# Second attention of a fused attention and two-layer-pair kernel: from one chunk at a time to sets of two or four chunks, turned by VectorE and DMAs

## The chip, the cores and the metric

The kernel runs on one core of a Trainium2 chip. The metric is the device time in microseconds (us). One launch computes everything; the host only lays the inputs out and turns the output back.

## The reference

All of it is float32, with N = 12480 tokens, C = 128 channels, 32 inducing vectors and FF = 2048. The inputs x, inducing, both matrices of the first pair and the first one of the second are drawn as below and multiplied by 8.

```python
def mab(q, kv):                       # attention without projections
    s = scale * (q @ kv.T); s = s - s.max(-1)
    a = exp(s); a /= a.sum(-1) + 1e-09
    return a @ kv
h = mab(inducing, x)                  # first attention: 32 rows over all tokens
x = mab(x, h)                         # second attention: every token over 32 rows
t = x @ w_in;  x = maximum(0.01*t, t) @ w_out            # first pair
t = x @ w_in2                                            # second pair
g = where(t >= 1, t, where(t <= -1, 0, (t + 1)**2 / 4))
y = g @ w_out2
```

## The kernel before, in words

Channels and hidden units lie on the 128 partitions, tokens along the free dimension. The first attention goes over all tokens in nine bands and ends at some 46 us with `HT`, the 32 rows, channel by row. Then the 12480 tokens are worked off in 25 chunks, ten of 504 and fifteen of 496 tokens (`WIDTHS`), and each chunk's 2048 hidden units in 16 blocks of 128 (`NJ`). A step k of the main loop is one such block, c, j = divmod(k, 16). The order of all instructions on each engine is the order in which the program is written.

In a step four stages stand beside each other, each for a block of its own:

- Stage 1 (while k < 400): one product `Gs` x `aT` for block k into a bank of `b1`. `aT` holds the second attention's weights of chunk c, 96 rows by tokens: low parts, high parts, high parts again (32 rows each). `Gs` is `HT` times the first matrix. ScalarE takes the high part (`hi`, L565), VectorE the low part (`lo`, L572); in four steps of sixteen GpSimd does the latter (L570), after a copy `r` by ScalarE.
- Stage 2, four steps behind: three products into `px` (bank 0 or 1 by the chunk's parity, `bX`). At the end of a chunk come one more product with `Qs` and the split into `x2hi` and `x2lo` (L619, L620).
- Stage 3, from k = 86 on, for block kb = k - 86: three products into one of the three banks `b3`. VectorE clamps (`cl`, L597), ScalarE squares (`sq`, L577), VectorE adds (`g`, L603), ScalarE takes the high part (L584) and GpSimd the low part (`lo`, L589).
- Stage 4, five blocks behind stage 3: three products into `py`; at a chunk's end a copy and a DMA to `out_y`.

So a step has 4 products for k < 86, 7 for k = 86 to 90, 10 up to k = 400, and 6 afterwards. All of these are issued by `mm` (L516). Before k = 86 (called the fill below) the weights of three matrices are converted as well, on VectorE, ScalarE and GpSimd (`convert`, L96 to L124).

The second attention of chunk c + 1 is made during chunk c by `attend`, one part at the end of each of some steps. Chunks 0 to 6 are scored by token: four products with the chunk's tokens as weights put 126 tokens on the partitions and 4 x 32 scores along them (L470, 4 products in 8 passes). Chunks 7 to 24 are scored by row (L448, likewise 8 passes), copied by ScalarE (L452) and turned by TensorE (L455). Then VectorE takes the maximum (L476) and the difference (L478), ScalarE the exponential (L481), VectorE sum, reciprocal and product (L485 to L488), ScalarE the high part (L492), VectorE the low part (L495), TensorE turns both in four products with an identity (L501), and ScalarE copies the turned rows out of PSUM (L506, L508). The bank is `bX[c % 2]`. `ATTEND` and `ATTEND_G` name the steps j of a chunk in which the parts stand. All DMAs go through the SP queue. At k = 86 the pools of the fill are closed and their memory is used by stages 3 and 4.

Of the kernel before, what the change touches and what calls it, by code (L numbers as in the profile page):

```python
# [31 lines left out]
SCALE = 1.0 / math.sqrt(C)  # L32
EPS = 1e-9
# [37 lines left out]
def moe_kernel(ctx: ExitStack, tc, x_d, xf_d, xl_d, xt_d, it_d, w1_d, w2_d, w3_d, w4_d, y_d):  # L71


    nc = tc.nc
# [8 lines left out]
    xp = ctx.enter_context(tc.tile_pool(name="xp", bufs=2))  # L83
    ps = ctx.enter_context(tc.tile_pool(name="ps", bufs=1, space=PSUM))
# [81 lines left out]

    xts = {}

    def load_xt(c):
        t = xp.tile([C, CW], F32, name="xt")  # L170
        nc.sync.dma_start(out=t[:, :WIDTHS[c]], in_=xt_d[:, AT[c]:AT[c + 1]])
        xts[c] = t

# [12 lines left out]
    xb, xT = {}, {}  # L186
# [24 lines left out]
    ident = const.tile([128, 128], F32, name="ident")  # L211
# [24 lines left out]
    HT = const.tile([C, 3, M], F32, name="HT")  # L236
# [85 lines left out]
    for s in range(NS_B):  # L322
# [14 lines left out]
        if s == NS_B - 3:  # L337
# [31 lines left out]
                            in1=rden[:, None, :].to_broadcast([C, 3, M]), op=ALU.mult)  # L369
# [9 lines left out]
    at = ctx.enter_context(tc.tile_pool(name="at", bufs=2))  # L379
    ap = ctx.enter_context(tc.tile_pool(name="ap", bufs=2))  # L380
# [3 lines left out]
    bX = (bank[0], bank[1])  # L384
# [3 lines left out]
    x2, h1, aT, st = {}, {}, {}, {}  # L388
# [49 lines left out]

    def scores_g(c, part):

        b = bX[c % 2]
        bt = WIDTHS[c] // CB
        if part == 0:
            t = xts.pop(c)
            if c + 1 < NCH:
                load_xt(c + 1)
            for q in range(CB):
                nc.tensor.matmul(b[q * M:(q + 1) * M, :bt], lhsT=HT[:, 0, :], rhs=t[:, q * bt:(q + 1) * bt],  # L448
                                 start=True, stop=True)
        elif part == 1:  # L450
            s = at.tile([128, BT], F32, name="sT")
            nc.scalar.activation(s[:, :bt], b[:, :bt], AF.Copy)  # L452
            st[c] = s[:, :bt]
        else:
            nc.tensor.transpose(b[:bt, 128:256], st[c], ident)  # L455

    def attend(c, part):

        b = bX[c % 2]
        bt = WIDTHS[c] // CB  # L460
        if c >= GROUPS:
            if part < 3:
                return scores_g(c, part)
            part -= 2
        if part == 0:
            t = xts.pop(c)
            if c + 1 < NCH:
                load_xt(c + 1)
            for q in range(CB):
                nc.tensor.matmul(b[:bt, q * M:(q + 1) * M], lhsT=t[:, q * bt:(q + 1) * bt], rhs=HT[:, 0, :],  # L470
                                 start=True, stop=True)
        elif part == 1:
            at0 = 128 if c >= GROUPS else 0
            sv = b[:bt, at0:at0 + CB * M].rearrange("p (b m) -> p b m", m=M)
            m = at.tile([BT, CB], F32, name="m")[:bt]
            nc.vector.tensor_reduce(out=m, in_=sv, op=ALU.max, axis=AX.X)  # L476
            e = at.tile([BT, CB, M], F32, name="ea")[:bt]
            nc.vector.tensor_tensor(out=e, in0=sv, in1=m[:, :, None].to_broadcast([bt, CB, M]), op=ALU.subtract)  # L478
            st[c] = e
        elif part == 2:  # L480
            nc.scalar.activation(st[c], st[c], AF.Exp, scale=SCALE)  # L481
        elif part == 3:
            e = st[c]
            d = at.tile([BT, CB], F32, name="d")[:bt]
            nc.vector.tensor_reduce(out=d, in_=e, op=ALU.add, axis=AX.X)  # L485
            nc.vector.tensor_scalar(out=d, in0=d, scalar1=EPS, scalar2=None, op0=ALU.add)
            nc.vector.reciprocal(out=d, in_=d)
            nc.vector.tensor_tensor(out=e, in0=e, in1=d[:, :, None].to_broadcast([bt, CB, M]), op=ALU.mult)  # L488
        elif part == 4:
            e = st[c]  # L490
            s = at.tile([BT, CB, 3, M], F32R, name="s")[:bt]
            nc.scalar.activation(s[:, :, 1, :], e, AF.Copy)  # L492
            if c == 0:
                nc.scalar.activation(s[:, :, 2, :], e, AF.Copy)
            nc.vector.tensor_tensor(out=s[:, :, 0, :], in0=e, in1=s[:, :, 1, :].bitcast(F32), op=ALU.subtract)  # L495
            st[c] = s
        elif part == 5:
            s = st.pop(c)
            r = 2 if c else 3
            for q in range(CB):  # L500
                nc.tensor.matmul(b[:r * M, q * bt:(q + 1) * bt], lhsT=s[:, q, :r].rearrange("p r m -> p (r m)"),  # L501
                                 rhs=identr[:bt, :bt], start=True, stop=True)
        elif part == 6:
            t = ap.tile([K1, CW], F32R, name="aT")[:, :CB * bt]
            r = 2 if c else 3
            nc.scalar.activation(t[:r * M], b[:r * M, :CB * bt], AF.Copy)  # L506
            if c:
                nc.scalar.activation(t[2 * M:], b[M:2 * M, :CB * bt], AF.Copy)  # L508
            aT[c] = t

    def mm(out, w, x, start, stop):

        n = x.shape[1]
        cuts = [n * i // PARTS for i in range(PARTS + 1)]
        for i, (a, b) in enumerate(zip(cuts, cuts[1:])):
            nc.tensor.matmul(out[:, a:b], lhsT=w, rhs=x[:, a:b], start=start and i == 0, stop=stop and i == PARTS - 1)  # L516

# [21 lines left out]
    work(WORK_T[3])  # L539

    NS = NCH * NJ
    for k in range(NS + LAG * NJ + OB + D2):
        c, j = divmod(k, NJ)
        kb = k - LAG * NJ - OB
        cb, jb = divmod(kb, NJ)
# [5 lines left out]
        if kb == 0:  # L551
# [4 lines left out]
            ep = ctx.enter_context(tc.tile_pool(name="ep", bufs=3))  # L556
        steps = ATTEND_G if c + 1 >= GROUPS else ATTEND
        part = steps.index(j) if j in steps and c + 1 < NCH else None
# [63 lines left out]
        if 0 <= ky < NS:  # L622
# [9 lines left out]
        if part is not None:  # L632
            attend(c + 1, part)
        if k in HIDDEN:
# [59 lines left out]
```

## Time and profile before

| | |
|---|---|
| time, median of 3 runs | 1009.83 us (1009.11 to 1010.76) |
| time of the profiled execution | 1012.33 us |
| its span, first to last instruction | 1010.5 us |
| TensorE busy, share of the span | 995.8 us, 99% |
| VectorE / ScalarE / GpSimd busy | 830.0 / 826.1 / 643.8 us |

The span is what the views of the profile show; 1.8 us of the profiled execution lie outside it. A product is shown longer than the time for which it holds TensorE, since the products overlap; the distance from the start of one to the start of the next tells what it costs.

### The profile page before, as it was taken

Reading aid. Unit: us, or ns where it says so; the run is one execution under the profiler, and the core shown is the slowest. Engines: PE = TensorE matmul, PEld = TensorE weight load, DVE = VectorE, ACT = ScalarE, POOL = GpSimd, SP = SyncE. Lnnn points to the kernel's source line nnn. Section 1 sums busy time; section 2 is a strip of 40 time slices with the busy share of each in tenths; the row PEclk is TensorE's granted clock in tenths of the full one; section 3 lists DMA queues with packets and bytes.
Section 4 is the critical chain, followed back from the end, with each engine's and each line's share of the span. In section 5 each row is a group of like instructions: output and inputs, shape, how many; then the busy total and the mean of one; then the engine's idle time right before and its main releaser. Section 6 shows DMA issues by size and latency. Waiting matters only on the chain.

```text
span 1010.5 us, 15224 instructions
## 1 busy us (share of the span) xinstructions
PE 995.8 (99%) x4858; PEld 806.2 (80%) x4858; DVE 830.0 (82%) x1442; ACT 826.1 (82%) x1556; POOL 643.8 (64%) x513
## 2 busy tenths in 40 slices
PE   8899999999999999999999999999999999999998
PEld 6567777888888888888888888888888888888886
DVE  5768998888888888888878878878878878789997
ACT  5577788888888888888888888888888888889987
POOL 0034466667667666666666666666666666678886
PEclk9999999999999999999999999999999999999999
DMA  9700000000000000000000000000000000000000
GB/s 357 311 15 11 21 12 11 12 10 21 14 8 21 18 4 21 22 1 21 21 1 22 21 1 21 20 1 21 21 1 21 12 1 11 11 11 11 11 11 21
DMA packets 11232, 29.86 MB, mean 30 GB/s; under 512 B 1376, under 2 KB 7776, under 8 KB 10384
## 3 DMA queue, kind: packets, MB, share of 16 engines
q1 hardware_dynamic: 11152, 28.89, 8.0%
q8 instruction: 38, 0.62, 0.3%
q14 instruction: 42, 0.34, 0.1%
HBM read 22.50 MB, written 6.39 MB: 29 GB/s over the span
## 4 chain that ended last, share of the span: by engine, by line
PE 93%; DVE 3%; ACT 2%; POOL 1%; issue 1%; POOLq 0%; ACTq 0%
PE bank L516 86%; PE bank L255 1%; ACT hi L565 1%; DVE lo L572 1%; PE bank L267 1%; PE bank L300 1%; PE bank L501 1%; PE bank L448 1%; PE bank L470 1%; DVE ea L488 0%; PE bank L318 0%; PE bank L225 0%; PE bank L395 0%; PE bank L289 0%; DVE cva L109 0%
## 5 line engine op out<-in xcount | busy, mean ns | idle before, releaser
L589 POOL TENSOR_TENSOR lo<-g,hi 128x496 fp32r<-128x496 f32 (+1 forms) x392 | 497.4, 1272 | 228.3 <-PE bank L516 162.1
L565 ACT ACTIVATE hi<-bank 128x496 fp32r<-128x496 f32 (+1 forms) x400 | 233.4, 590 | 122.6 <-PE bank L516 119.8
L516 PE MATMUL bank<-lo,whi 128*128 128x496 f32 (+1 forms) x800 | 310.4, 388 | 1.5 <-POOL lo L570 1.5
L516 PE MATMUL bank<-hi,whi 128*128 128x496 f32 (+1 forms) x800 | 310.7, 388 | 0.0
L516 PE MATMUL bank<-hi,wlo 128*128 128x496 f32 (+1 forms) x800 | 310.3, 388 | 0.0
L577 ACT ACTIVATE sq<-cl,half 128x496 f32<-128x496 f32 (+1 forms) x400 | 284.2, 711 | 12.3 <-DVE cl L597 5.5
L597 DVE TENSOR_SCALAR cl<-bank 128x496 f32<-128x496 f32 (+1 forms) x400 | 268.2, 670 | 27.6 <-PE bank L516 22.0
L603 DVE SCALAR_TENSOR_TENSOR g<-bank,sq 128x496 f32<-128x496 f32 (+1 forms) x400 | 267.8, 669 | 25.7 <-ACT sq L577 24.2
L572 DVE SCALAR_TENSOR_TENSOR lo<-bank,hi 128x496 fp32r<-128x496 f32 (+1 forms) x305 | 203.7, 674 | 92.8 <-ACT hi L565 92.7
L584 ACT ACTIVATE hi<-g 128x496 fp32r<-128x496 f32 (+1 forms) x400 | 245.7, 614 | 0.7 <-DVE g L603 0.5
L516 PEld LDWEIGHTS bank<-lo,whi 128*128 128x128 f32 x800 | 150.3, 188 | 34.2 <-POOL lo L570 3.2
L516 PEld LDWEIGHTS bank<-hi,wlo 128*128 128x128 f32 x800 | 150.5, 188 | 30.2
L516 PEld LDWEIGHTS bank<-hi,whi 128*128 128x128 f32 x800 | 150.5, 188 | 30.0 <-ACT y L630 0.4
L516 PE MATMUL bank<-aT,Gs 96*128 96x496 f32 (+1 forms) x400 | 164.1, 411 | 0.8 <-ACT aT L506 0.8
L570 POOL TENSOR_TENSOR lo<-r,hi 128x496 fp32r<-128x496 f32 (+1 forms) x95 | 122.9, 1294 | 64.9 <-ACT r L569 61.3
L516 PE MATMUL bank<-x2hi,whi 128*128 128x496 f32 (+1 forms) x400 | 156.1, 390 | 0.7 <-DVE g L603 0.7
L516 PE MATMUL bank<-x2hi,wlo 128*128 128x496 f32 (+1 forms) x400 | 155.4, 389 | 0.0
L516 PE MATMUL bank<-x2lo,whi 128*128 128x496 f32 (+1 forms) x400 | 155.2, 388 | 0.0
L516 PEld LDWEIGHTS bank<-aT,Gs 96*128 96x128 f32 x400 | 75.3, 188 | 21.2 <-issue 4.5
L516 PEld LDWEIGHTS bank<-x2hi,wlo 128*128 128x128 f32 x400 | 75.9, 190 | 14.9
L516 PEld LDWEIGHTS bank<-x2hi,whi 128*128 128x128 f32 x400 | 75.9, 190 | 14.4 <-DVE g L603 1.5
L516 PEld LDWEIGHTS bank<-x2lo,whi 128*128 128x128 f32 x400 | 75.2, 188 | 15.3
(120 smaller groups left out, 537.7 us busy)
## 6 DMA issues: line engine op xcount, KB each, us to landing
wraw<-in_w SPq DMA_DIRECT2D x16, 512.0 KB, 9.9
xb<-in_x SPq DMA_DIRECT2D x5, 1024.0 KB, 14.2
xt<-in_xt SPq DMA_DIRECT2D x15, 248.0 KB, 2.7
out_y<-y SPq DMA_DIRECT2D x15, 248.0 KB, 2.0
xt<-in_xt SPq DMA_DIRECT2D x10, 252.0 KB, 2.7
out_y<-y SPq DMA_DIRECT2D x10, 252.0 KB, 2.1
xl<-in_xl SPq DMA_DIRECT2D x1, 1024.0 KB, 15.2
xb<-in_x SPq DMA_DIRECT2D x2, 256.0 KB, 8.4
```

The source lines that it names most:

```text
L255: nc.tensor.transpose(ps_t[:, i * p:(i + 1) * p], xb[s][:, q, b, :], ident[:p, :p])
L267: nc.tensor.matmul(p[q * M:(q + 1) * M, :w], lhsT=iT, rhs=xT[s][:, q * w:(q + 1) * w], start=True, stop=True)
L300: nc.tensor.matmul(A[q * M:(q + 1) * M], lhsT=eTs[s][:p, b * 128 + q * M:b * 128 + (q + 1) * M], rhs=xb[s][:, q, b, :], start=(b == 0), st ...
L516: nc.tensor.matmul(out[:, a:b], lhsT=w, rhs=x[:, a:b], start=start and i == 0, stop=stop and i == PARTS - 1)
L565: nc.scalar.activation(hi, p1, AF.Relu)
L570: nc.gpsimd.tensor_tensor(out=lo, in0=r, in1=hi.bitcast(F32), op=ALU.subtract)
L572: nc.vector.scalar_tensor_tensor(out=lo, in0=p1, scalar=0.0, in1=hi.bitcast(F32), op0=ALU.max, op1=ALU.subtract)
L577: nc.scalar.activation(sq, cl, AF.Square, scale=-0.5, bias=half)
L584: nc.scalar.activation(hi, g, AF.Copy)
L589: nc.gpsimd.tensor_tensor(out=lo, in0=g, in1=hi.bitcast(F32), op=ALU.subtract)
L597: nc.vector.tensor_scalar(out=cl, in0=p3, scalar1=1.0, scalar2=-1.0, op0=ALU.min, op1=ALU.max)
L603: nc.vector.scalar_tensor_tensor(out=g, in0=b3[(kb - 1) % 3][:, :w], scalar=-1.0, in1=sq, op0=ALU.max, op1=ALU.add)
```

## The change

The first three chunks (0 to 2) are still scored by token, one at a time. The other 22 are done in seven sets: two of 2 chunks, four of 4 and one of 2. A set's part p stands at the end of step first + p, for p from 0 to 11. The scores are made by row for the whole set, four products of n x 128 columns. VectorE turns them in blocks of 32 x 32 out of PSUM, so that each partition holds tokens and 32 scores lie next to each other. Maximum, difference, sum and product are done on n x 128 elements a partition, now from SBUF, the exponential and the high part by ScalarE; high and low parts are turned back by the same kind of VectorE instruction, and twelve DMAs a set (SBUF to SBUF, 32 partitions and runs of 125 floats each) spread them into the 96 rows of `aTg`. TensorE turns nothing in a set, and ScalarE copies nothing out of PSUM.

Chunks are now 488, 496, 496 and 22 times 500 tokens. The x of a set is laid out by the host in quarters of 128 tokens (125 and the next three) and loaded in one DMA, of 1 MB for four chunks. The set of step 89 is loaded at k = 86, into memory of the fill. Chunks 1 and 2 have their high parts copied twice by ScalarE before the turn, as chunk 0 had, and so one copy out of PSUM.

```diff
-WIDTHS = (504,) * 10 + (496,) * 15
+WIDTHS = (488, 496, 496) + (500,) * 22
+TB = 128
+SINGLE = 3
+SETS = ((3, 2, 15), (5, 2, 36), (7, 4, 89), (11, 4, 150), (15, 4, 214), (19, 4, 278), (23, 2, 342))
+PARTS = 12
+FEW, MANY = 2, 4
...
+    def attend_set(i, part):
+        c, n, k = SETS[i]
+        b = bX[(k // NJ + 1) % 2]
+        w = n * TB
...
+        def spread(t, r, v):
+            v = v.rearrange("p (n t) -> p n t", t=TB)
+            for q in range(CB):
+                nc.sync.dma_start(out=t[r * M:(r + 1) * M, :n, q * bt:(q + 1) * bt].bitcast(F32),
+                                  in_=v[q * M:(q + 1) * M, :, :bt])
+        if part == 0:
+            t = xts.pop(c)
+            for q in range(CB):
+                nc.tensor.matmul(b[q * M:(q + 1) * M, :w], lhsT=HT[:, 0, :], rhs=t[:, :, q, :], start=True, stop=True)
+            if i + 1 < len(SETS) and (late_pools or SETS[i + 1][2] < kb0):
+                load_xt(*SETS[i + 1][:2])
+        elif part == 1:
+            nc.vector.transpose(out=e, in_=b[:, :w])
+        elif part == 2:
+            nc.vector.tensor_reduce(out=m, in_=blocks(st[c]), op=ALU.max, axis=AX.X)
+        elif part == 3:
+            nc.vector.tensor_tensor(out=blocks(e), in0=blocks(e), in1=wide(m), op=ALU.subtract)
+        elif part == 4:
+            nc.scalar.activation(st[c], st[c], AF.Exp, scale=SCALE)
+        elif part == 5:
+            nc.vector.tensor_reduce(out=d, in_=blocks(e), op=ALU.add, axis=AX.X)
+            nc.vector.tensor_scalar(out=d, in0=d, scalar1=EPS, scalar2=None, op0=ALU.add)
+            nc.vector.reciprocal(out=d, in_=d)
+        elif part == 6:
+            nc.vector.tensor_tensor(out=blocks(e), in0=blocks(e), in1=wide(d), op=ALU.mult)
+        elif part == 7:
+            nc.scalar.activation(hi, st[c], AF.Copy)
+        elif part == 8:
+            nc.vector.transpose(out=hT, in_=hi.bitcast(F32))
+        elif part == 9:
+            for r in (1, 2):
+                spread(t, r, hT)
+        elif part == 10:
+            nc.vector.tensor_tensor(out=lo, in0=e, in1=hi.bitcast(F32), op=ALU.subtract)
+            nc.vector.transpose(out=lT, in_=lo.bitcast(F32))
+        else:
+            spread(t, 0, lT)
...
+        for i, (_, _, first) in enumerate(SETS):
+            if 0 <= k - first < PARTS:
+                attend_set(i, k - first)
```

## Rows read from the trace of the kernel before

**Rows 1.** The page, chain that ended last, shares of the span by engine.

```profile
PE 93%; DVE 3%; ACT 2%; POOL 1%; issue 1%; POOLq 0%; ACTq 0%
```

**Rows 2.** Busy time by engine, one chunk of the fill, one later chunk.

```profile
core 0: us, PE busy (x) PEld busy (x) DVE busy (x) ACT busy (x) POOL busy (x), PEclk, DMA share, GB/s
92.76:110.51 17.75, 16.97 (x78) 13.08 (x78) 17.08 (x30) 13.86 (x29) 9.76 (x7) 1.00 0.06 16
211.26:249.00 37.74, 37.74 (x175) 30.62 (x174) 30.85 (x53) 31.58 (x60) 25.40 (x21) 1.00 0.05 15
```

**Rows 3.** TensorE in order of time, steps of ten products: start, duration, line.

```profile
500.50 0.39 PE L516 MATMUL bank<-lo,whi 128*128 128x504 f32 x1
500.97 0.40 PE L516 MATMUL bank<-x2hi,whi 128*128 128x504 f32 x1
...
505.06 0.39 PE L516 MATMUL bank<-lo,whi 128*128 128x504 f32 x1
505.82 0.40 PE L516 MATMUL bank<-x2hi,whi 128*128 128x504 f32 x1
...
563.36 0.39 PE L516 MATMUL bank<-lo,whi 128*128 128x496 f32 x1
564.36 0.39 PE L516 MATMUL bank<-x2hi,whi 128*128 128x496 f32 x1
...
568.40 0.38 PE L516 MATMUL bank<-lo,whi 128*128 128x496 f32 x1
568.96 0.39 PE L516 MATMUL bank<-x2hi,whi 128*128 128x496 f32 x1
```

**Rows 4.** TensorE in order of time, scores of the first attention.

```profile
24.77 1.04 PE L267 MATMUL bank<-xT,iT 128*32 128x512 f32 x8
25.74 0.66 PE L289 MATMUL bank<-ident,e 128*128 128x128 f32 x4
```

**Rows 5.** Groups by line and shape, VectorE: busy us, mean ns, idle before.

```profile
L495 DVE TENSOR_TENSOR s<-ea,s 124x128 fp32r<-124x128 f32 x15 | 20.8, 1387 | 0.0
...
L608 DVE TENSOR_TENSOR lo<-g,hi 128x496 fp32r<-128x496 f32 x8 | 5.3, 667 | 0.2 <-ACT hi L584 0.2
...
L488 DVE TENSOR_TENSOR ea<-ea,d 124x128 f32<-124x128 f32 x15 | 4.4, 292 | 0.5
```

**Rows 6.** All engines in order of time, end of a step of ten products.

```profile
573.24 1.26 POOL L589 TENSOR_TENSOR lo<-g,hi 128x496 fp32r<-128x496 f32 x1 [1.05 <-PE bank L516]
573.26 0.67 DVE L603 SCALAR_TENSOR_TENSOR g<-bank,sq 128x496 f32<-128x496 f32 x1
...
575.49 0.39 PE L516 MATMUL bank<-aT,Gs 96*128 96x496 f32 x1
```

**Rows 7.** All engines in order of time, steps of the fill.

```profile
98.32 0.39 PE L516 MATMUL bank<-aT,Gs 96*128 96x504 f32 x1
...
98.85 0.67 DVE L620 TENSOR_TENSOR x2lo<-bank,x2hi 128x504 fp32r<-128x504 f32 x1
...
99.58 1.07 PE L470 MATMUL bank<-HT,xt 128*126 128x32 f32 x8 [0.17 <-DVE x2lo L620]
100.48 0.48 PE L516 MATMUL bank<-aT,Gs 96*128 96x504 f32 x1
...
105.14 0.40 PE L516 MATMUL bank<-aT,Gs 96*128 96x504 f32 x1
...
106.05 0.39 PE L516 MATMUL bank<-aT,Gs 96*128 96x504 f32 x1
...
107.64 0.45 PE L516 MATMUL bank<-aT,Gs 96*128 96x504 f32 x1
...
151.49 0.39 PE L516 MATMUL bank<-lo,whi 128*128 128x504 f32 x1
...
152.51 0.47 PE L516 MATMUL bank<-aT,Gs 96*128 96x504 f32 x1
```

**Rows 8.** The page, DMA issues: count, size, median us from issue to landing.

```profile
xt<-in_xt SPq DMA_DIRECT2D x15, 248.0 KB, 2.7
```

More of the change, by code (lines that the diff above doesn't have):

```diff
@@ L167, in moe_kernel, with load_xt @@
     xts = {}
[L169 to L172, printed above, removed]
+    late_pools = {}
+    def load_xt(c, n=1):
+        if n == 1:
+            t = xp.tile([C, CB * TB], F32, name="xt", bufs=2)
+        elif n == FEW and not late_pools:
+            t = xp.tile([C, FEW * CB * TB], F32, name="xts")[:, :n * CB * TB]
+        else:
+            t = late_pools["x"].tile([C, MANY * CB * TB], F32, name="xtm")[:, :n * CB * TB]
+        nc.sync.dma_start(out=t, in_=xt_d[:, c * CB * TB:(c + n) * CB * TB])
+        xts[c] = t.rearrange("p (n q t) -> p n q t", q=CB, t=TB)
     iT = const.tile([C, M], F32, name="iT")
@@ L437, in linear, with tile_of, blocks, wide @@
             nc.vector.tensor_tensor(out=lo, in0=b[M:2 * M, :C], in1=lo.bitcast(F32), op=ALU.subtract)
-    def scores_g(c, part):
+    def attend_set(i, part):
+        c, n, k = SETS[i]
+        b = bX[(k // NJ + 1) % 2]
+        pool = late_pools["a"] if late_pools else at
+        most = MANY if late_pools else FEW
+        w = n * TB
+        bt = WIDTHS[c] // CB
+        def tile_of(name, dtype=F32):
+            return pool.tile([128, most * TB], dtype, name=name)[:, :w]
+        def blocks(t):
+            return t.rearrange("p (b m) -> p b m", m=M)
+        def wide(t):
+            return t[:, :, None].to_broadcast([128, n * CB, M])
+        def spread(t, r, v):
[10 more added lines that the diff above has]
+        elif part == 1:
+            e = tile_of("eg")
+            nc.vector.transpose(out=e, in_=b[:, :w])
+            st[c] = e
+        elif part == 2:
+            m = pool.tile([128, most * CB], F32, name="mg")[:, :n * CB]
+            nc.vector.tensor_reduce(out=m, in_=blocks(st[c]), op=ALU.max, axis=AX.X)
+            st[c] = st[c], m
+        elif part == 3:
+            e, m = st[c]
+            nc.vector.tensor_tensor(out=blocks(e), in0=blocks(e), in1=wide(m), op=ALU.subtract)
+            st[c] = e
+        elif part == 4:
+            nc.scalar.activation(st[c], st[c], AF.Exp, scale=SCALE)
+        elif part == 5:
+            e = st[c]
+            d = pool.tile([128, most * CB], F32, name="dg")[:, :n * CB]
+            nc.vector.tensor_reduce(out=d, in_=blocks(e), op=ALU.add, axis=AX.X)
+            nc.vector.tensor_scalar(out=d, in0=d, scalar1=EPS, scalar2=None, op0=ALU.add)
+            nc.vector.reciprocal(out=d, in_=d)
+            st[c] = e, d
+        elif part == 6:
+            e, d = st[c]
+            nc.vector.tensor_tensor(out=blocks(e), in0=blocks(e), in1=wide(d), op=ALU.mult)
+            st[c] = e
+        elif part == 7:
+            hi = tile_of("hg", F32R)
+            nc.scalar.activation(hi, st[c], AF.Copy)
+            st[c] = st[c], hi
+        elif part == 8:
+            e, hi = st[c]
+            hT = tile_of("hT")
+            nc.vector.transpose(out=hT, in_=hi.bitcast(F32))
+            st[c] = e, hi, hT
+        elif part == 9:
+            e, hi, hT = st[c]
+            t = (late_pools["t"] if late_pools else ap).tile([K1, most, CW], F32R, name="aTg")
+            for r in (1, 2):
+                spread(t, r, hT)
+            st[c] = e, hi, t
+        elif part == 10:
+            e, hi, t = st[c]
+            lo = tile_of("lg", F32R)
+            nc.vector.tensor_tensor(out=lo, in0=e, in1=hi.bitcast(F32), op=ALU.subtract)
+            lT = tile_of("lT")
+            nc.vector.transpose(out=lT, in_=lo.bitcast(F32))
+            st[c] = lT, t
+        else:
+            lT, t = st.pop(c)
+            spread(t, 0, lT)
+            for i in range(n):
+                aT[c + i] = t[:, i, :]
@@ L441, in scores_g, with attend @@
+    def attend(c, part):
         b = bX[c % 2]
@@ L444, in scores_g @@
             t = xts.pop(c)
-            if c + 1 < NCH:
+            if c + 1 < SINGLE:
                 load_xt(c + 1)
+            if c == 0:
+                load_xt(*SETS[0][:2])
             for q in range(CB):
-                nc.tensor.matmul(b[q * M:(q + 1) * M, :bt], lhsT=HT[:, 0, :], rhs=t[:, q * bt:(q + 1) * bt],
+                nc.tensor.matmul(b[:bt, q * M:(q + 1) * M], lhsT=t[:, 0, q, :bt], rhs=HT[:, 0, :],
                                  start=True, stop=True)
         elif part == 1:
[L451 to L474, printed above, removed]
+            sv = b[:bt, :CB * M].rearrange("p (b m) -> p b m", m=M)
             m = at.tile([BT, CB], F32, name="m")[:bt]
@@ L498, in attend @@
             s = st.pop(c)
-            r = 2 if c else 3
             for q in range(CB):
-                nc.tensor.matmul(b[:r * M, q * bt:(q + 1) * bt], lhsT=s[:, q, :r].rearrange("p r m -> p (r m)"),
+                nc.tensor.matmul(b[:K1, q * bt:(q + 1) * bt], lhsT=s[:, q].rearrange("p r m -> p (r m)"),
                                  rhs=identr[:bt, :bt], start=True, stop=True)
         elif part == 6:
[L504 to L508, printed above, removed]
+            t = ap.tile([K1, CW], F32R, name="aT0")[:, :CB * bt]
+            nc.scalar.activation(t, b[:K1, :CB * bt], AF.Copy)
             aT[c] = t
     def mm(out, w, x, start, stop):
[L513 to L516, printed above, removed]
+        nc.tensor.matmul(out, lhsT=w, rhs=x, start=start, stop=stop)
     def mm3(out, n, j, hi, lo, start, stop):
@@ L539, in moe_kernel @@
     work(WORK_T[3])
+    kb0 = LAG * NJ + OB
     NS = NCH * NJ
@@ L556, in moe_kernel @@
             ep = ctx.enter_context(tc.tile_pool(name="ep", bufs=3))
-        steps = ATTEND_G if c + 1 >= GROUPS else ATTEND
-        part = steps.index(j) if j in steps and c + 1 < NCH else None
+            for name in ("x", "a"):
+                late_pools[name] = ctx.enter_context(tc.tile_pool(name="late_" + name, bufs=1))
+            late_pools["t"] = ctx.enter_context(tc.tile_pool(name="late_t", bufs=2))
+            load_xt(*next(g for g in SETS if g[2] > k)[:2])
         if in_a:
@@ L631, in moe_kernel @@
                 nc.sync.dma_start(out=y_d[:, AT[cy]:AT[cy + 1]], in_=y)
-        if part is not None:
-            attend(c + 1, part)
+        if c + 1 < SINGLE and j in ATTEND:
+            attend(c + 1, ATTEND.index(j))
+        for i, (_, _, first) in enumerate(SETS):
+            if 0 <= k - first < PARTS:
+                attend_set(i, k - first)
         if k in HIDDEN:
@@ L670, in band @@
         return t.reshape(G4, -1, p, C).transpose(2, 0, 1, 3).reshape(p, -1)
+    xT = np.zeros((C, N + TB), x.dtype)
+    xT[:, :N] = x.reshape(N, C).T
+    blocks = np.concatenate([xT[:, AT[c] + q * w // CB:AT[c] + q * w // CB + TB]
+                             for c, w in enumerate(WIDTHS) for q in range(CB)], axis=1)
     laid = {
```

16 lines of the change are left out of this document (6 added, 10 removed).

## The prediction

> **What bounds the kernel now.** First I read the chain of waits: TensorE carries 93% of it, so what counts is how long TensorE is held, and by what it is made to wait [rows 1]. Next the busy times by stretch, which show two regimes [rows 2]. From step 91 to 399 a chunk takes 37.74 us in which TensorE never pauses, while VectorE is busy 30.85 and ScalarE 31.58: only what is taken off TensorE's own queue shortens it. In the fill a chunk takes 17.75 us with VectorE at 17.08, and TensorE pauses for 0.8: there VectorE has nothing to spare. Last I read TensorE in order of time, since its products overlap and the cost of an insertion is the distance of the starts around it.
>
> **What is removed from TensorE, step 91 on.** From the last product of a step to the second of the next it is 0.47 us (500.50 to 500.97). With the scores between them it is 1.00 (563.36 to 564.36): 0.53 more. With the turn of the copied scores it is 0.56 (0.09 more), with the four products that turn the weights 0.76 (0.29 more) [rows 3]. That makes 0.91 us a chunk; chunks 7 to 24 are 18, so 16.4 us. Chunk 6 is attended at k = 85 and after: its scores by token cost 1.02 from last product to next first, less the usual 0.23, so 0.79 [rows 7], and with 0.29 for the turn 1.1. Removed: 17.5 us.
>
> **What is added to it there.** Four products of 32 x 512 for a set of four. The nearest row is the scores of the first attention, the same shape: 0.97 us to the start of the next group (24.77 to 25.74) [rows 4]. That is the lower end; the upper is four times 0.53, if nothing is gained by width. I take 1.15, the row and the 0.18 by which 0.53 exceeds the 0.35 us that the present scores occupy between starts, my estimate. A set of two I put halfway between 0.53 and 1.15, at 0.74. Four sets of four and one of two: 5.3 us. Net from step 85 on: -17.5 + 5.3 = -12.2 us.
>
> **The fill.** A plain step is 0.91 us (105.14 to 106.05); the one with the turn 1.59, since TensorE also waits for VectorE's low part: 0.68 more. The step with chunk 3's scores is 2.16 (98.32 to 100.48), 1.25 more, some of it a wait for `x2lo` [rows 7]. Chunks 3, 4 and 5 therefore cost 1.25 + 0.79 + 0.79 + 3 x 0.68 = 4.9 us, and all that goes. In come two sets of two, 1.5 us. The second stands at k = 36, one step earlier than chunk 3's scores did, in the bank from which `x2lo` of chunk 1 is just being taken: `x2lo` ends at 99.52, and step 36 has issued its products by 98.32, so TensorE waits 1.2 us there, with the next step's products queued behind it. Net: -4.9 + 1.5 + 1.2 = -2.2 us. VectorE's work in the fill grows by some 2 us: two sets of eight instructions of 0.48, halfway between the two sizes [rows 5], and three waits for GpSimd (below), 5.5 us each, against three chunks of 2.9 (five instructions of 0.29, two small ones, one wait of 1.1). It moves to steps 15 to 47, where it may come late by up to 3 us, a bound; the steps after have nothing of it.
>
> **VectorE in a set.** A set of four has on VectorE eight instructions of 512 elements and two small ones. The row nearest in size is 667 ns (`lo`, two SBUF inputs), and 128 elements take 292 (`L488`) [rows 5]. The block transpose is in no row; it is bounded below by 0.67 and above by four times 0.29 = 1.2, and I take 0.67, since it moves as many elements one by one. A step leaves VectorE idle: 30.85 less 3 of attention is 27.9 for 16 steps, or 1.9 us in the twelve steps with `lo`, 1.27 in the four without. At 2.26 us a step (573.23 to 575.49) 0.36 is idle in the former and 0.99 in the latter. So a 512-wide part puts VectorE behind by 0.3 us, the double part at the end by 1.0.
>
> On top comes a wait. `L495`, 128 elements from two SBUF inputs, takes 1387 ns in each chunk of 496, against 292 for its like: it stands still while GpSimd works on its own two SBUF inputs. Three instructions of a set are of that kind. They follow `g` directly; GpSimd's `lo` starts with `g` and lasts 1.26, so 0.57 of it is left when `g` ends [rows 6]. With 0.57 each, VectorE's delay runs in steps 8 to 16 of the set's chunk as 0.3, 1.2, 0.9, 1.1, 2.0, 1.6, 2.0, 1.0, 2.5 us. What is late next: stage 3's products of step k + 2 need the bank that `g` reads; they start at 575.72 where `g` ends at 573.93, so 1.8 us are free. The largest delay passes that by 0.75: four sets, 3 us; I take 2, since back-to-back VectorE instructions start closer than they last. Bounds: 0 without the waits, 9 with 1.1 us for each (largest delay 4.05).
>
> The Trainium skill (SBUF — State Buffer, section "SBUF: two separate sides") says that VectorE with two SBUF inputs and GpSimd take one pair of ports by an exclusive lock for a whole instruction, whoever starts first, and that the other stands still. The 1387 ns agree. By that rule a wait may be as long as one whole GpSimd instruction, and GpSimd in turn may be held for a whole VectorE instruction; that is the rival *Less* below.
>
> The skill (VectorE: DVE Perf Modes, section "The three transpose paths") gives 311 ns for VectorE's transpose of 128 x 128 in bf16. By four of these a 512-wide transpose would be an estimated 1.24 us, and the sum some 5 us higher; no row here shows it.
>
> **What costs nothing.** ScalarE loses five instructions a chunk and gains two a set; it is not the bound, and its slack grows. The twelve DMAs: they begin at parts 9 and 11, the last at k = 100 for chunk 7, which begins at k = 112: 12 steps, 27 us; the others have 15 and more, or 22 in the fill. A load of 248 KB lands in 2.7 us [rows 8]; twelve of at most 64 KB each, one behind the other, by the same price 32 us at worst, so only the first set of four could be late at all, by 5; taken as none. On SP they stand between y's stores, which have no one waiting for them but the buffer after next. The 1 MB load for k = 89: between 2.7 and four times that, 10.8 us; from k = 86 to the end of step 89 it is about 6.4, but SP waits for no product and can issue it as soon as its memory is free. I take 0, bound 4.4. Widths: the columns are the same in all, about 1 us less in the fill, 0.9 more at the end. Transposes, copies and waits of the first three chunks: unchanged within 1 us.
>
> **The sum.** -12.2 - 2.2 + 2 = -12.4 us. The profiled execution has a span of 1010.5 and took 1012.3; by the sum they become 998.1 and 999.9. The median of the runs is 1009.8, so 997.4. That case by itself reaches from 992 (no VectorE stall, no wait at k = 36) to 1002 (VectorE's delay in the fill not absorbed, or the 1 MB load late): 66 in 100.
>
> **The rivals.**
>
> - *More.* The pauses of TensorE in the fill go as well, 0.8 us a chunk over three chunks, since VectorE and ScalarE have less to do there, and neither VectorE's stall nor the wait at k = 36 comes: 997.4 - 2.4 - 2 - 1.2 = 991.8 and below. For it: VectorE at 17.08 of 17.75 [rows 2]. Against: the conversions, which share VectorE and GpSimd, stay. 8 in 100.
> - *Less.* The waits for GpSimd are 1.1 each, or the transpose takes 1.2: 7 or 5 us above the sum, 1002 to 1005. For it: the 1387 ns. Against: `L488`, two SBUF inputs as well, shows no wait in fifteen chunks [rows 5], and the delay can be made up in steps without `lo`. 17 in 100.
> - *Slower.* The delays of VectorE are not absorbed at all: each part's excess goes to TensorE. One set of four has 0.3 + 0.9 + 0.2 + 0.9 + 0.3 + 1.6 = 4.2 us of it; four and a half sets 19, in place of 2: 997.4 + 17 = 1014. It decides from 3.2 us a set. For it: 82% of VectorE and only two banks for stage 1. Against: the 1.8 us that `g` has free [rows 6]. 6 in 100.
> - *No change.* The set's weights land too late, so that TensorE waits at each set's first chunk for about what it saves, 2.8 us; needs a DMA some ten times slower than the rows show. 3 in 100.
>
> Anything under 0.2% (2 us) a measurement of this kernel can hardly tell from no change. Faster 0.90, same 0.03, slower 0.07. For 8 in 10 I take 990 to 1003.
>
> **What would show it.** Right: after step 91 chunks of 36.7 us or so, TensorE without a pause; the scores of a set 1.1 us; no `PE` instruction between `aT` and VectorE; step 36 with a wait for `x2lo` of about 1.2; chunks from k = 48 to 80 near 15.6 us, where the row of the fill has 17.75. Wrong: 512-wide transposes well over 0.7 us; VectorE's three instructions with two SBUF inputs at 1.7 us and more; TensorE idle in steps 8 to 17 of a set with a releaser on VectorE (`g`, `cl`) or waiting on a DMA at k = 89, 112 or 176.

## The result, and the profile after

The changed kernel takes 999.8 us (median of 4, 999.0 to 1000.6), the kernel before beside it 1010.3: a ratio of 0.9892, 95% interval 0.9868 to 0.9916. A second measurement on another occasion gave 999.1 and 0.9879 (0.9865 to 0.9892). That is faster by 10.5 and 12.4 us in the medians, or 11 to 12 by the ratios, where 12.4 were forecast; 997.4 was the time forecast, with 990 to 1003 around it. The profiled execution has a span of 997.2 us, with 1.8 us outside it as before; the two spans differ by 13.3 us, of which about 1 us, before step 0, goes with the clock (below).

The table cuts the two spans at the starts of stage 1's product (`aT`, now `aTg`, with `Gs`) of steps 0, 16, 86, 91 and 399, read from TensorE in order of time. The third line is the same changed kernel profiled again: it shows what such a number is worth. From step 16 on it repeats within 0.1 us. The first five steps differ by 0.9, and there TensorE's granted clock differs: in the first profile of the changed kernel it is at 1.2 GHz, the lower of its two levels, from 50.4 to 53.8 us, in the second at 2.4 GHz throughout. The kernel before was at 1.2 GHz from 52.9 to 56.3 us, and from 8.6 to 12.0 as well. The three profiles of all runs that have the earlier of these stretches reach step 0 at 51.6 us, the others at 49.9 to 51.1. So the first two columns are no measure of the change.

```
                 to step 0   0-16   16-86   86-91   91-399   after 399    span
before              51.64   23.24   77.63    8.17   720.94      128.88  1010.5
changed             50.64   23.52   76.52    9.17   706.90      130.47   997.2
changed, again      50.70   22.63   76.49    9.17   706.94      130.37   996.3
```

The gain lies where TensorE never paused: 14.0 us in steps 91 to 399, less 1.0 in steps 86 to 91, where the scores of a set of four have come in. The fill gives back 1.1 us in steps 16 to 86, and the last stretch costs 1.5 to 1.6. The page's chain says the same in one line, to be held against [rows 1]:

```profile
PE 94%; DVE 3%; ACT 1%; POOL 1%; issue 0%; ACTq 0%; POOLq 0%
```

Busy times by stretch: a chunk of the fill (steps 32 to 48), a chunk with no set in it (112 to 128), and all of steps 16 to 86. They answer to [rows 2].

```profile
core 0: us, PE busy (x) PEld busy (x) DVE busy (x) ACT busy (x) POOL busy (x), PEclk, DMA share, GB/s
93.56:112.29 18.73, 16.15 (x74) 12.05 (x73) 17.34 (x30) 13.27 (x27) 9.69 (x7) 1.00 0.03 8
207.27:243.68 36.41, 36.41 (x162) 30.31 (x161) 28.10 (x46) 29.73 (x55) 25.10 (x21) 1.00 0.02 8
74.16:150.68 76.52, 70.24 (x318) 54.78 (x315) 70.78 (x122) 57.95 (x114) 40.15 (x29) 1.00 0.11 31
```

The chunk of 37.74 us has become one of 36.41, and TensorE is still busy without a pause: it had less to do. The same chunk of the fill went from 17.75 to 18.73, and in it TensorE is busy 16.15 where it was 16.97: it has less to do there too, and waits for more. VectorE is at 17.34, hardly idle, as before.

The scores of a set of four, TensorE in order of time at step 150; they answer to [rows 3]:

```profile
296.05 0.39 PE L577 MATMUL bank<-lo,whi 128*128 128x500 f32 x1
296.37 1.07 PE L474 MATMUL bank<-xtm,HT 128*32 128x512 f32 x8
297.37 0.49 PE L577 MATMUL bank<-aTg,Gs 96*128 96x500 f32 x1
297.70 0.39 PE L577 MATMUL bank<-x2hi,whi 128*128 128x500 f32 x1
```

From the last product of the step to the second of the next it is 1.65 us, where it is 0.47 without a set: 1.18 us more for four chunks. The estimate was 1.15.

VectorE's instructions in sets of four, groups by line and shape (busy us, mean ns of one, idle before):

```profile
L520 DVE TENSOR_TENSOR lg<-eg,hg 128x512 fp32r<-128x512 f32 x4 | 4.4, 1091 | 0.0
...
L487 DVE TENSOR_TENSOR eg<-eg,mg 128x512 f32<-128x512 f32 x4 | 3.9, 971 | 0.0
L500 DVE TENSOR_TENSOR eg<-eg,dg 128x512 f32<-128x512 f32 x4 | 3.8, 954 | 0.0
...
L479 DVE STREAM_TRANSPOSE eg<-bank 128x512 f32<-128x512 f32 x4 | 2.8, 707 | 0.0
L509 DVE STREAM_TRANSPOSE hT<-hg 128x512 f32<-128x512 f32 x4 | 2.8, 705 | 0.0
```

A block transpose of 512 columns takes 0.71 us from PSUM and from SBUF alike, the value taken having been 0.67. The three instructions with two SBUF inputs take 0.95 to 1.09 in the mean, in place of 0.67, so they wait for GpSimd by 0.3 to 0.4 us each in the mean, not by 0.57. The means hide two cases. `L500` takes 0.68 in three of the sets, with no GpSimd instruction beside it, and 1.77 in the first, where one had begun 0.02 us earlier. `L487` and `L520` take 0.78 to 1.15; there GpSimd had begun 0.65 to 1.04 us earlier, so only the rest of its instruction was left to wait for. One of the two small instructions (`L495`) waits as well, 0.60 us in place of 0.17 in three sets.

In the fill TensorE waits at three places that the kernel before did not have, or had shorter; TensorE in order of time, steps 28, 34 and 36:

```profile
89.93 0.53 PE L569 MATMUL bank<-identr,s 124*96 124x124 f32 x4 [1.05 <-DVE s L564]
...
97.49 0.49 PE L577 MATMUL bank<-lo,whi 128*128 128x496 f32 x1 [1.29 <-POOL lo L634]
...
101.11 0.64 PE L474 MATMUL bank<-xts,HT 128*32 128x256 f32 x8 [1.10 <-DVE x2lo L684]
```

The first is the turn of chunk 2, late because VectorE works on the first set in the same steps; the third is the wait for `x2lo` that was forecast at 1.2. The second is a low part on GpSimd. What holds it up is seen on GpSimd and VectorE in order of time:

```profile
94.50 1.29 POOL L126 TENSOR_TENSOR wlo<-cva,cvb 128x512 fp32r<-128x512 f32 x1 [3.57 <-DVE cvb L118]
95.76 1.68 POOL L634 TENSOR_TENSOR lo<-r,hi 128x496 fp32r<-128x496 f32 x1
97.40 1.29 POOL L125 TENSOR_TENSOR cva<-cva,whi 128x512 f32<-128x512 f32 x1
...
100.09 1.48 POOL L634 TENSOR_TENSOR lo<-r,hi 128x496 fp32r<-128x496 f32 x1
```

```profile
89.70 1.52 DVE L520 TENSOR_TENSOR lg<-eg,hg 128x256 fp32r<-128x256 f32 x1
...
97.43 1.54 DVE L109 TENSOR_SCALAR cvb<-wraw 128x512 uint32<-128x512 uint32 x1
...
100.06 0.41 DVE L109 TENSOR_SCALAR cvb<-wraw 128x512 uint32<-128x512 uint32 x1
```

GpSimd's queue stands 3.57 us at a weight conversion whose input VectorE has not yet made; the low part comes after it. VectorE in turn loses up to 1.1 us when one of its SBUF instructions finds GpSimd already at work: `L109` takes 1.54 at 97.43, where GpSimd had begun at 97.40, and 0.41 at 100.06, where GpSimd began after it, at 100.09.

### The profile page after: what moved, and what is told of

Its sections match the earlier page's. It is cut to its first block, busy times and chain, and to the rows that moved or that the text cites. A ratio compares the mean times of both kernels' runs of the same rounds, so it can differ in the third digit from the quotient of the medians.

```text
span 997.2 us, 14764 instructions
## 1 busy us (share of the span) xinstructions
PE 979.1 (98%) x4632; PEld 795.9 (80%) x4632; DVE 811.1 (81%) x1358; ACT 799.3 (80%) x1464; POOL 643.4 (65%) x513
## 4 chain that ended last, share of the span: by engine, by line
PE 94%; DVE 3%; ACT 1%; POOL 1%; issue 0%; ACTq 0%; POOLq 0%
PE bank L577 89%; DVE lo L636 1%; PE bank L263 1%; PE bank L275 1%; PE bank L308 1%; PE bank L474 1%; PE bank L233 0%; ACT hi L629 0%; PE bank L326 0%; PE bank L297 0%; PE bank L403 0%; POOL lo L634 0%; DVE cvb L118 0%; POOL wlo L126 0%; DVE cva L111 0%
## 5 line engine op out<-in xcount | busy, mean ns | idle before, releaser
L653 POOL TENSOR_TENSOR lo<-g,hi 128x500 fp32r<-128x500 f32 (+2 forms) x392 | 496.3, 1269 | 205.7 <-PE bank L577 152.0
L629 ACT ACTIVATE hi<-bank 128x500 fp32r<-128x500 f32 (+2 forms) x400 | 234.5, 588 | 135.7 <-PE bank L577 131.6
L577 PE MATMUL bank<-lo,whi 128*128 128x500 f32 (+2 forms) x800 | 311.3, 389 | 3.6 <-POOL lo L634 3.1
L577 PE MATMUL bank<-hi,whi 128*128 128x500 f32 (+2 forms) x800 | 311.1, 389 | 0.0
L577 PE MATMUL bank<-hi,wlo 128*128 128x500 f32 (+2 forms) x800 | 310.4, 388 | 0.0
L661 DVE TENSOR_SCALAR cl<-bank 128x500 f32<-128x500 f32 (+2 forms) x400 | 268.3, 671 | 43.6 <-PE bank L577 37.5
L641 ACT ACTIVATE sq<-cl,half 128x500 f32<-128x500 f32 (+2 forms) x400 | 284.4, 711 | 17.9 <-DVE cl L661 11.3
L667 DVE SCALAR_TENSOR_TENSOR g<-bank,sq 128x500 f32<-128x500 f32 (+2 forms) x400 | 268.0, 670 | 35.0 <-ACT sq L641 34.8
L636 DVE SCALAR_TENSOR_TENSOR lo<-bank,hi 128x500 fp32r<-128x500 f32 (+2 forms) x305 | 203.7, 672 | 76.8 <-ACT hi L629 76.3
L648 ACT ACTIVATE hi<-g 128x500 fp32r<-128x500 f32 (+2 forms) x400 | 245.7, 614 | 0.5 <-DVE g L667 0.5
L577 PEld LDWEIGHTS bank<-x2lo,whi 128*128 128x128 f32 x400 | 75.2, 188 | 15.4
## 6 DMA issues: line engine op xcount, KB each, us to landing
aTg<-hT SPq DMA_DIRECT2D x32, 62.5 KB, 2.0
xl<-in_xl SPq DMA_DIRECT2D x1, 1024.0 KB, 15.4
aTg<-lT SPq DMA_DIRECT2D x16, 62.5 KB, 2.0
```

The source lines that it names most:

```text
L577: nc.tensor.matmul(out, lhsT=w, rhs=x, start=start, stop=stop)
L629: nc.scalar.activation(hi, p1, AF.Relu)
L636: nc.vector.scalar_tensor_tensor(out=lo, in0=p1, scalar=0.0, in1=hi.bitcast(F32), op0=ALU.max, op1=ALU.subtract)
L641: nc.scalar.activation(sq, cl, AF.Square, scale=-0.5, bias=half)
L648: nc.scalar.activation(hi, g, AF.Copy)
L653: nc.gpsimd.tensor_tensor(out=lo, in0=g, in1=hi.bitcast(F32), op=ALU.subtract)
```

## The experiments

All stretches below are cut as in the table above. Ratios are to the kernel before, measured beside it on the same chip. Some expectations give steps 0 to 91; since the first steps vary with the clock, as shown above, the results compare steps 16 to 91.

**The changed kernel again**, for the numbers to compare with.

> The changed kernel once more, on the same chip as the next three, for a number to compare them with. All theories: 0.989 of the kernel before, some 999.8 us; steps 0 to 91 take 109.2 us as in its profile.

Measured: 999.1 us, ratio 0.9879 (0.9865 to 0.9892); steps 16 to 91 85.7 us, steps 0 to 91 108.3.

**Where in the fill the two sets stand.** My theory A was that the first set collides with chunk 2's own attention; theory B that VectorE has too much to do in the fill wherever it stands.

```diff
-SETS = ((3, 2, 15), (5, 2, 36), ...
+SETS = ((3, 2, 30), (5, 2, 56), ...
```

> The two sets of the fill begin at steps 30 and 56 in place of 15 and 36; nothing else. Theory A: in the fill the gain is lost because the first set's VectorE work stands in the same steps as chunk 2's own attention (21 to 29), so that VectorE falls behind and TensorE waits at steps 28, 30, 34 and 36; apart from each other, the sets cost only their scores. Then steps 0 to 91 take about 105.5 us (109.2 before this edit), step 28 no more than 1.6, and the time is some 3.5 us below the changed kernel's, 996.3. Theory B: VectorE's total work in the fill is what is too much, wherever it stands; then steps 0 to 91 stay at 109 and the time at 999.8, with the waits moved to steps 40 to 70.

Measured: 1004.6 us, ratio 0.9934 (0.9922 to 0.9947), some 5 us slower than the changed kernel, which neither theory expected. Step 28 falls to 1.76 us and step 34 to 0.93, as A has it, but steps 39 to 46 gain waits, and step 47 takes 5.58. Of the 6.8 us that steps 16 to 91 take more, step 47 has 4.1. There TensorE waits for the DMAs of the first set (SP's queue, then TensorE, in order of time):

```profile
102.67 5.83 SPq L468 DMA_DIRECT2D aTg<-hT  x8
108.60 2.50 SPq L468 DMA_DIRECT2D aTg<-lT  x4
```

```profile
112.87 0.76 PE L577 MATMUL bank<-aTg,Gs 96*128 96x500 f32 x1 [3.76 <-DMA aTg<-lT]
```

Each issue holds SP for 0.6 us (the first two here 0.7 and 1.2), so twelve take 8.4 from the first to the end of the last, and the last lands 1.9 us after its issue: from 102.67 to 112.4. This set needed 9.7 us between VectorE's turned high parts and its first chunk, and had less. The clock adds to it: TensorE stopped at 109.1 us, its granted clock was at 1.2 GHz from 110.5 to 117.4, and steps 48 and 49 take 1.79 and 1.66 us in place of 0.98 and 1.02, 1.4 us more in both.

```diff
-SETS = ((3, 2, 15), (5, 2, 36), ...
+SETS = ((3, 2, 15), (5, 2, 56), ...
```

> Only the second set of the fill is moved, from step 36 to 56. Theory A: the wait for x2lo at step 36 (1.1 us) goes, and the lateness at steps 47 to 51 with it; the waits at steps 28, 30 and 34 stay. Steps 0 to 91 about 107.5 us, time some 998. Theory B: no change, 109 and 999.8.

Measured: 998.7 us, ratio 0.9872 (0.9859 to 0.9886). Steps 36, 47, 50 and 66 are shorter by 4.2 us in all, but steps 56, 67, 72, 73 and 82 are longer by as much, in waits and scores; steps 16 to 91 take 85.2 us in place of 85.7 (steps 0 to 91 108.8). Most of the waits have moved with the set, which is theory B.

```diff
-WIDTHS = (488, 496, 496) + (500,) * 22
-SINGLE = 3
-SETS = ((3, 2, 15), (5, 2, 36), ...
+WIDTHS = (496,) * 5 + (500,) * 20
+SINGLE = 5
+SETS = ((5, 2, 56), ...
```

> Chunks 3 and 4 are attended one at a time as chunks 0 to 2 are, and only chunks 5 and 6 make a set in the fill, from step 56; the first five chunks are 496 wide. Theory A: the first set's waits (steps 19, 28, 30, 34, 36) go, but chunks 3 and 4 bring back scores of 0.8 and turns of 0.7 each: steps 0 to 91 about 106.5 us, time some 997. Theory B: VectorE's work is about the same, so 109 and 999.8.

Measured: 998.6 us, ratio 0.9875 (0.986 to 0.989). Steps 16 to 91 take 87.1 us, 1.5 more (steps 0 to 91 109.2); steps 0 to 16 lose the scores at step 15. Sets or single chunks make no difference to the time, as B has it: again the waits changed places.

**Taking VectorE's work away in the same steps.**

```diff
         elif part == 3:
             e, m = st[c]
-            nc.vector.tensor_tensor(out=blocks(e), in0=blocks(e), in1=wide(m), op=ALU.subtract)
+            if late_pools:
+                nc.vector.tensor_tensor(out=blocks(e), in0=blocks(e), in1=wide(m), op=ALU.subtract)
```

(The VectorE instructions of parts 2, 5 and 6 likewise. The kernel leaves the softmax of chunks 3 to 6 out, but for the exponential.)

> The two sets of the fill leave out maximum, difference, sum, reciprocal and product (for chunks 3 to 6 the exponentials of the bare scores are used): 2.1 us of VectorE's work less in each, in the same steps. Theory B (VectorE's total work bounds the fill): steps 16 to 91 shrink by the whole 4.2 us, from 85.7 to about 81.5, and the time to 995.5. Theory A (only the collision with chunk 2's attention costs): at most 2 us, from steps 28, 30 and 34. Third: the fill is bound by GpSimd's low parts or by TensorE; no change.

Measured: 996.4 us, ratio 0.9858 (0.9841 to 0.9875); steps 16 to 91 82.6 us, 3.1 less. Steps 28 and 50 lose 1.9 us, but 34 and 36 nothing. It is more than A allowed and less than the full 4.2 of B.

**GpSimd's share of the low parts in the fill**, one more and then one less.

```diff
-POOL_LO1_FILL = (3, 9, 14)
+POOL_LO1_FILL = (2, 6, 10, 14)
```

> In the fill four low parts of sixteen are done by GpSimd (steps 2, 6, 10, 14) in place of three (3, 9, 14), so VectorE has one instruction of 0.6 us less a chunk, ScalarE a copy more and GpSimd 1.3 us more. Theory B: steps 16 to 91 shrink by some 2.6 us and the time to about 997. Rival: VectorE's instructions with two SBUF inputs or in the fast SBUF mode wait for GpSimd by as much again; no change or worse.

Measured: 1000.8 us, ratio 0.9904 (0.9889 to 0.9919); steps 16 to 91 87.8 us, 2.1 more. The rival had it, no change or worse: VectorE has one instruction less a chunk and is busy for 2.1 us longer. Two things besides the number differ here. The steps themselves moved, and TensorE, after a wait of 1.6 us for `x2lo`, was at 1.2 GHz from 100.4 to 103.8 us, where steps 37 and 38 take 1.72 and 1.65 in place of 1.00 and 0.90: 1.5 of the 2.1 us. The interval touches that of the changed kernel, so that this version is slower is not shown; that it doesn't gain the 2.6 us of theory B is.

```diff
-POOL_LO1_FILL = (3, 9, 14)
+POOL_LO1_FILL = (3, 9)
```

> The other way from the last edit: in the fill GpSimd does the low parts of steps 3 and 9 of sixteen alone, step 14 goes back to VectorE. In the changed kernel TensorE waits three times, 3.1 us in all, for GpSimd's low part of a step 14, which stands on GpSimd behind a conversion that waits for VectorE. Theory B (the fill goes by VectorE's busy time, its waits for GpSimd included): VectorE gains 0.6 us of work a chunk and loses a wait of about 1.2, so steps 16 to 91 shrink by some 2 to 3 us, from 85.7 to 83, and the time to 997. Rival: VectorE's own work is what counts and its waits for GpSimd stay: 2.6 us longer, 88 and 1002.

Measured: 997.0 us, ratio 0.9847 (0.9832 to 0.9861); steps 16 to 91 83.5 us, 2.2 less. VectorE has one instruction more a chunk and is busy for less. Step 34 is plain (0.90 for 2.44), step 66 too; step 51 takes 2.74 for 1.36. Here the number alone changed, and the clock stood at 2.4 GHz throughout the stretch.

```diff
-SETS = ((3, 2, 15), (5, 2, 36), ...
+SETS = ((3, 2, 15), (5, 2, 56), ...
-POOL_LO1_FILL = (3, 9, 14)
+POOL_LO1_FILL = (3, 9)
```

> The edit before and the second set of the fill begun at step 56 in place of 36, which by itself took 0.5 us off steps 16 to 91. Theory B: steps 16 to 91 at 82 to 83 us, time some 996.5, below both kernels. Rival: as before, 87 and 1001.

Measured: 995.4 us, ratio 0.9840 (0.9828 to 0.9853), the fastest of all; steps 16 to 91 82.0 us. Its interval lies below both of the changed kernel's, so this version beats both kernels. In steps 16 to 91 it saves 3.7 us, while the low part moved back gives 2.2 by itself and the set moved 0.5: together they give more than singly.

In the kernel before, the last line of that edit alone:

```diff
-POOL_LO1_FILL = (3, 9, 14)
+POOL_LO1_FILL = (3, 9)
```

> The kernel before the change with the same edit of GpSimd's low parts (steps 3 and 9 of sixteen in the fill). If VectorE's waits for GpSimd bound the fill already before the change, its steps 16 to 86 shrink from 77.6 us by 2 to 3 as well and its time to some 1007.5; if that is a matter of the changed kernel's sets alone, nothing or 2 us longer.

Measured: 1008.8 us, ratio 0.9966 (0.9953 to 0.9979); steps 16 to 86 74.8 us in place of 77.6. So GpSimd's share cost time in the fill before the change as well. With the same two low parts the change is worth as much as with three, 0.9847 against 0.9966.

Busy times of steps 16 to 86, the columns as above, one line from each kernel: the one before,

```profile
74.88:152.51 77.63, 74.96 (x354) 58.70 (x352) 70.37 (x124) 60.13 (x122) 40.19 (x29) 1.00 0.05 14
```

without the softmax in the fill,

```profile
74.23:147.65 73.42, 69.44 (x319) 54.96 (x316) 66.66 (x110) 57.58 (x114) 40.23 (x29) 1.00 0.12 33
```

four low parts on GpSimd,

```profile
72.75:151.39 78.64, 72.67 (x319) 55.87 (x316) 72.84 (x118) 59.42 (x118) 44.92 (x33) 0.98 0.11 31
```

two of them,

```profile
74.45:148.82 74.37, 69.63 (x319) 54.91 (x316) 68.49 (x126) 55.91 (x110) 34.80 (x25) 1.00 0.11 32
```

and two of them in the kernel before.

```profile
72.36:147.13 74.77, 73.92 (x355) 58.87 (x352) 68.44 (x128) 58.04 (x118) 35.31 (x25) 1.00 0.06 15
```

The stretch (second number) less VectorE's busy time (fourth) is 7.3, 6.8, 5.8, 5.9 and 6.3 us; for the changed kernel it is 5.7, with its second set moved 5.9, with one set in the fill 6.3. Two runs lie outside. With both sets later it is 12.0, where TensorE waits for DMAs and has the lower clock afterwards. In the fastest version it is 3.6:

```profile
75.27:148.06 72.79, 69.90 (x318) 54.84 (x316) 69.17 (x126) 55.54 (x110) 34.00 (x25) 1.00 0.11 32
```

Against the version with two low parts only the place of the second set differs; VectorE is busy 0.7 us longer, and the stretch is 1.6 us shorter. So VectorE's busy time, which holds its waits for GpSimd, goes with the length in most of these runs, but it is not the whole of it: the place of a set counts too. TensorE's busy time runs from 69.4 to 75.0 and doesn't go with the length by itself. From the kernel before to the changed one it fell by 4.7 us, and TensorE's idle time rose from 2.7 to 6.3.

How much of VectorE's busy time is waiting can be estimated from the traces: over steps 16 to 86, what its instructions last beyond the fastest of the same line and shape (counted where it is over 0.1 us) adds up to 9.0 us in the changed kernel, 15.4 with four low parts on GpSimd and 5.4 with two; in the kernel before to 6.3, and 1.4 with two.

**TensorE's part alone, after the fill.**

```diff
+        if in_a and j == 12 and 7 <= c + 1 < NCH:
+            free = bX[(c + 1) % 2]
+            nc.tensor.transpose(free[:124, 128:256], ident[:, :124], ident)
+            for q in range(CB):
+                nc.tensor.matmul(free[:64, q * 124:(q + 1) * 124], lhsT=identr[:124, :64], rhs=identr[:124, :124],
+                                 start=True, stop=True)
```

> TensorE does one transpose of 124 columns and four products of 64 x 124 with an identity again in step 12 of chunks 6 to 23, into the bank that is free there; nothing reads them. It is TensorE's part of the turns alone, without the copies by ScalarE and without a wait for them. Theory: the gain after step 85 is TensorE's own time and nothing else; then each of 18 chunks grows by 0.09 + 0.29 us and the time by 6.8 us, to some 1006. Rival: the gain is one of waits and of ScalarE's copies; then the time grows by less than 2 us.

Measured: 1007.3 us, ratio 0.9966 (0.9954 to 0.9979); steps 91 to 399 take 714.0 us, 7.1 more, or 0.39 for each of 18 chunks, where 0.38 were worked out. The time of TensorE's turns is gained one for one.

**VectorE's slack, after the fill.**

```diff
         elif part == 8:
-            nc.vector.transpose(out=hT, in_=hi.bitcast(F32))
+            for _ in range(2 if late_pools else 1):
+                nc.vector.transpose(out=hT, in_=hi.bitcast(F32))
```

(Parts 1 and 10 likewise.)

> In the sets after step 86 each of the three VectorE block transposes is done twice, 0.7 us more at parts 1, 8 and 10. Theory: VectorE's delay in a set is absorbed up to the 1.8 us that the bank of g has free; with the measured waits the largest delay is now just under that, with the doubled transposes 3.4 us, so TensorE stands still for 1 to 1.6 us in each set of four and the time grows by 4 to 7 us. Rival: there is far more slack than 1.8 us, since VectorE was never the reason for anything after step 91; then the time grows by less than 1 us. Second rival: nothing is absorbed; then 2.1 us for each set, over 9 us.

Measured: 1003.9 us, ratio 0.9931 (0.9914 to 0.9949); steps 91 to 399 take 711.3 us, 4.3 more. All of it is one wait in each set of four, 1.05 us in three of them and 1.2 in the first, none in the set of two. VectorE and TensorE in order of time, after the last double transpose:

```profile
326.59 0.66 DVE L670 SCALAR_TENSOR_TENSOR g<-bank,sq 128x500 f32<-128x500 f32 x1
```

```profile
327.31 0.50 PE L580 MATMUL bank<-x2hi,whi 128*128 128x500 f32 x1 [0.68 <-DVE g L670]
```

(Without a pause one such product starts 0.23 to 0.33 us after the one before, here 1.17; the bracket counts only the 0.68 in which TensorE showed nothing, since instructions overlap.) It is the wait that the prediction named as the next to come: stage 3's product for the bank that `g` reads.

## Why the prediction came out

The mechanism after step 85 was right. That the total came so near, 12.4 us forecast and 11 to 12 measured, is in part luck: three of its terms were off and made up for each other.

- **TensorE after step 85** (-12.2 forecast, -13.5 measured in steps 85 to 399; right, and a little short). The set's scores cost 1.18 us where 1.15 was taken; the set of two adds 0.65 to step 342 and 0.1 to the next, 0.75 in all, where 0.74 was taken. That 0.74 is luck: it was called halfway between 0.53 and 1.15, which is 0.84. The turns cost 0.39 a chunk where they were put at 0.38, shown by putting them back. The stretch from step 91 fell by 14.0 us and contains three sets of four and one of two, 4.3 us, so 18.3 went. Of these, 0.91 a chunk explains 16.4 and chunk 6's turn 0.3. Another 1.08 is a wait in step 91 of the kernel before that the sum did not count, for `g` while VectorE did the attention of chunk 6 (TensorE in order of time, the kernel before):

```profile
161.86 0.49 PE L516 MATMUL bank<-x2hi,whi 128*128 128x504 f32 x1 [0.68 <-DVE g L603]
```

  That step fell from 3.33 to 2.25 us. Some 0.5 us is left over, 0.03 a chunk.

- **VectorE's stalls in the sets** (+2 forecast, bounds 0 to 9; none measured). The mechanism was right and the term too large. With waits of 0.3 to 0.4 in the mean in place of 0.57 TensorE paused in no set, so the delay stayed under the 1.8 us that `g` has free. Doubling the transposes passed that, and the stall came at the place and in the size that the reckoning gave, 1.05 to 1.2 against 1 to 1.6. The transposes at 0.71 bear out the lower bound. The Trainium skill (VectorE: DVE Perf Modes, section "The three transpose paths") gives 311 ns for 128 x 128 in bf16; four of these made an estimated 1.24 us, and the trace does not agree: a single instruction of 512 float32 columns takes 0.71. One reading was too kind: against the rival *Less* stood that `L488` shows no wait in fifteen chunks. Of the other ten, four in the fill take 1.38 to 1.40 us, GpSimd having begun 0.04 us before (VectorE, the kernel before, by line and shape):

```profile
L488 DVE TENSOR_TENSOR ea<-ea,d 126x128 f32<-126x128 f32 x10 | 7.3, 730 | 0.3
```

- **The fill** (-2.2 forecast; -0.7 from step 16 to the start of step 85. Step 85 itself, where the first term takes off 0.8 for chunk 6's scores, fell by 0.4 more, from 1.72 to 1.29, since TensorE now waits there for a low part of VectorE's.) Here a step of the working failed: removed and added items were counted on TensorE's queue, in a stretch of which the same text said that VectorE has nothing to spare [rows 2]. The items themselves were right: steps 53, 60, 69 and 76 became plain, the wait for `x2lo` came. TensorE was busy 4.7 us less in steps 16 to 86, but it stood idle for 3.6 us more; VectorE was busy 70.4 us before and 70.8 after. What TensorE no longer does turned into waits elsewhere (steps 28, 34, 36, 50). Less VectorE work (the run without softmax, -3.1 us) and fewer of its waits for GpSimd (two low parts, -2.2 us) do shorten the stretch. Theory A, the collision of the first set alone, with which I began, fell as the whole account. But theory B is not the whole of it either: with two low parts on GpSimd the place of the second set is worth 1.6 us. What else sets the length of the fill, and why TensorE stands idle in it for 2.9 us and more in every version of the changed kernel, is not settled.

- **The last stretch** (+0.9 forecast, 1.5 to 1.6 measured). It has chunks of 500 in place of 496; 0.9 of it is columns. The rest was not followed up.

- **What was put at nothing.** ScalarE: right. The 1 MB load lands in 4.8 us and nothing waits for it. The twelve DMAs were put at 32 us at worst, by 2.7 each one behind the other; they take 9 to 9.7, since they overlap but for 0.6 us of issue each. In the changed kernel every set has 18 us and more from its last issue to its first chunk, so the rival *No change* did not occur; moving the first set 15 steps later showed that it can, with a wait of 3.8 us.

```profile
aTg<-hT SPq DMA_DIRECT2D x32, 62.5 KB, 2.0
```

(The page's DMA issues: count, size, median us to landing.)

## What to carry to other kernels

In each stretch of a kernel count an edit on the engine that bounds that stretch: here the same edit was worth its full 0.4 us a turn where TensorE never paused, and a small part of it in the fill, where VectorE was busy for nine tenths of the time, however plainly TensorE's queue got shorter. Here an engine that is 80% busy took bursts for nothing up to the slack of the first buffer that waits for it, and that slack could be read off one step of the trace. Before giving an engine's work to another one, see whether the two can run at the same time at all. And look up the granted clock of a stretch before explaining a difference in it.

## What the runs showed of the hardware

- VectorE's waits for GpSimd are not confined to instructions with two SBUF inputs. Bit operations with one SBUF input and a constant (`L109`, `L113`, 512 columns) take 0.39 to 0.43 us, or up to 1.55 where GpSimd had begun before them; where they began first they take 0.41 with GpSimd beside them. In steps 16 to 86 one instruction a chunk moved from VectorE to GpSimd made VectorE busier by 2.1 us, and one moved back less busy by 2.3. The Trainium skill (SBUF — State Buffer, section "SBUF: two separate sides") names a VectorE instruction in a two-port mode beside one with two SBUF inputs as what takes the exclusive lock; the trace agrees as far as the times go.
- VectorE's block transposes do not wait for GpSimd: from SBUF, with GpSimd's instruction begun 0.84 to 0.86 us before and running on for 0.4, all four of `L509` at 512 columns take 0.70 to 0.71 us (VectorE, then GpSimd, in order of time).

```profile
317.43 0.71 DVE L509 STREAM_TRANSPOSE hT<-hg 128x512 f32<-128x512 f32 x1
```

```profile
316.57 1.26 POOL L653 TENSOR_TENSOR lo<-g,hi 128x500 fp32r<-128x500 f32 x1 [1.08 <-ACT hi L648]
```

- TensorE's clock fell to 1.2 GHz behind pauses in two of the runs: for 3.4 us with four low parts on GpSimd, behind a wait of 1.6 us, and for 6.8 us with both sets later, beginning 1.4 us after TensorE had stopped. Products of 496 columns then start 0.41 us apart in place of 0.23.
- A DMA from SBUF to SBUF of 32 partitions and runs of 500 bytes holds the issuing queue for 0.6 us and lands 1.8 to 2.1 us after its issue in the changed kernel, whether it has 31 or 62.5 KB.
- A float32 block transpose on VectorE takes 0.71 us for 512 columns, no longer out of PSUM than out of SBUF.
